# Scores and exponentials of an attention kernel in steps of 504 columns over chunk and pair borders

## The chip, the cores and the metric

One Trainium2 chip; the kernel runs on one core. The metric is the device time of one execution in microseconds (us). Engine names as the profile has them: PE is TensorE's matmul side and PEld its weight loads, DVE is VectorE, ACT is ScalarE, POOL is GpSimd, SP is SyncE. PSUM is the memory that PE writes and DVE and ACT read.

## The reference

```python
def _attn_ref(q, k, v):                      # (8, 8, 1152, 64) each
    q_pool = q.reshape(B, H, S // 2, 2, D).mean(axis=3)       # 576 pooled queries
    scores = scale * np.matmul(q_pool, k.transpose(0, 1, 3, 2))
    scores = scores - np.max(scores, axis=-1, keepdims=True)
    attn = np.exp(scores)
    attn = attn / (np.sum(attn, axis=-1, keepdims=True) + 1e-09)
    return np.matmul(attn, v)

def _moe_ref(x, domain_id, w1, w2):          # x: (4608, 512), 8 experts
    for e in range(E):
        mask = domain_id == e
        h = np.maximum(x[mask] @ w1[e], 0.0)
        out[mask] = h @ w2[e]
```

Attention over 64 heads, each with 576 pooled queries and 1152 keys of depth 64; its output is the token table `x` (4608 tokens of 512), and each token goes through the two-layer network of the one expert that `domain_id` names.

## The kernel before

Heads are worked in 32 pairs. The keys of a head form 9 chunks of 128, so a pair has 9 x 576 = 5184 columns of scores for each of its two heads (a column is one query against a chunk's 128 keys, which lie on the partitions). The two heads of a pair use the two halves of PE's rows (depth 64 each), and their matmuls run side by side.

**Steps.** A pair's 5184 columns are cut into 12 steps of W = 432. `score(t)` writes step t of both heads into one of three PSUM buffers `s0`, `s1`, `s2`, taken in turn by `next_s`; `expo(t)` is one ACT instruction that reads 2 x 432 columns and writes exponentials in f16 to a tile `e`. A tile `e` holds four steps, which are three chunks; four such tiles rotate (12 chunks). There are 32 x 12 = 384 steps, two to a window.

**Products.** `av(p, h, c)` is one unit of the second product: five matmuls with 128 columns of `e` as weights and 65 columns of values moving (the 65th sums the exponentials). Units go in the order pair, head, chunk, 576 in all. Nine units fill one accumulator `acc`, of which there is one in PSUM; after the ninth, `evac` empties it on DVE with a reciprocal and a multiplication, and the first unit of the next head waits for that.

**Turns.** `turn(p + 1)` transposes the next pair's keys and queries on PE (30 small matmuls with depth 64) into one of the same three buffers, and three DVE copies bring them to `kq` and `qz`. In the source it stands between the two scores of a window, at step 8 of pairs 0 and 1 and at step 4 of the later ones.

**The rest of the loop.** t counts steps of 432 columns. At fixed t or fixed t within the pair the loop also issues the loads of later pairs, the copies that prepare keys, queries and values on DVE (`prep_k`, `prep_q`, `prep_v`), a queue of small DVE operations `rq` that computes where each token goes (with a budget in ns for every step of a pair, `ROOM`), gathers of finished tokens on POOL (at the steps in `GET`), and weight loads. From t = 108 the products, and pieces of the first expert tiles, stand in an order written out by hand: `PLAN` has a word for each window, `A3` for three units, `P4` for four pieces of expert work, and a `/` where the second score of the window stands. A piece is four matmuls of the first layer, one of the second, or a tile's transposes; its PSUM tile `px` is single. Before t = 108 each window from t = 8 on has three units.

**After the loop.** At t = 384 the last 12 units are done, then the remaining expert tiles are computed by PE with ACT and DVE emptying PSUM, gathers and scatters on POOL, and, for the last runs, transposes by DMA on SP.

Of the kernel before, what the change touches and what calls it, by code (L numbers as in the profile page):

```python
# [19 lines left out]
def kernel(  # L20
# [50 lines left out]
    ering = att.enter_context(tc.tile_pool(name="ering", bufs=4))  # L71
# [13 lines left out]
    v16 = [pair.tile([P, NC, 2, DV], F16, name=f"v16_{i}") for i in range(NV)]  # L85
    ident = perm.tile([P, P], FP32, name="ident")
# [138 lines left out]
    sc = [perm.tile([P, E, PADC + NT], FP32, name=f"sc{i}") for i in range(2)]  # L225
# [321 lines left out]
    def prep_v(p):  # L547
        nc.vector.tensor_copy(  # L548
            v16[p % NV][:, :, :, 0:D].rearrange("p c h d -> p h c d"), loaded[p]["vs"][:, :, :, :]
        )  # L550
# [40 lines left out]
    st, et, acc, xb = {}, {}, {}, {}  # L591

    def score(t):
        p, s_ = divmod(t, SPP)
        s = next_s()
        st[t] = s
        o, u = 0, W * s_
        while o < W:
            c, q0 = divmod(u + o, Sp)
            n = min(Sp - q0, W - o)  # L600
            for r, (lo, hi) in enumerate(HALF):
                nc.tensor.matmul(  # L602
                    s[:, r, o : o + n], lhsT=kq[p][lo:hi, c * P : (c + 1) * P],
                    rhs=qz[p % 2][lo:hi, q0 : q0 + n], start=True, stop=True,
                )
            o += n

    def expo(t):
        p, s_ = divmod(t, SPP)
        if s_ % 4 == 0:  # L610
            et[p, s_ // 4] = ering.tile([P, 2, 4 * W], F16, name="e")
        e_ = et[p, s_ // 4]
        o = W * (s_ % 4)
        nc.scalar.activation(  # L614
            e_[:, :, o : o + W], st.pop(t)[:, :, 0:W], AF.Exp, bias=0.0, scale=0.0625
        )

    def av(p, h, c, pool):
        if c == 0:
            if pool[0] is spsum:  # L620
                acc[p, h] = next_s()[:, 0, :]
            else:
                acc[p, h] = pool[0].tile([P, 512], FP32, name=pool[1])
        for i in range(NQ):
            o = (c % 3) * Sp + QO[i]
            nc.tensor.matmul(  # L626
                acc[p, h][:, i * (D + 1) : (i + 1) * (D + 1)],
                lhsT=et[p, c // 3][:, h, o : o + P], rhs=v16[p % NV][:, c, h, 0 : D + 1],
                start=c == 0 and i == 0, stop=c == NC - 1, skip_group_check=True,
            )  # L630
# [18 lines left out]
    ends, cut = (nc.sync, nc.gpsimd), []  # L649

    def put_x(b, i):
        for lo, hi in zip(CUT, CUT[1:]):
# [19 lines left out]
    def get_x(pool, e, i):  # L672
        x_ = pool.tile([P, Dm], F16, name="xs")
        mark(x_[0:1, 0:1], True)
        nb = [ib // NQ for k_, ib in zip(KO[1:], IB) if (i + 1) * P <= k_] + [B]
        gather(x_[:, :], grow[:, e * NTC + i : e * NTC + i + 1], nb[0])
        xs[e, i] = x_
# [11 lines left out]
    def load_part(e, j):  # L689
# [7 lines left out]
    PLAN0 = 108  # L697
    PLAN = (
        "A3 A6 A/A A/- A4 A2 "
        "A3 A6 A/A2 P P4A A2P4 "  # L700
        "A6 P3A3 A3 A2/PA P4A A4P "
        "A4P2 P2A5 P2 A2/A2 P2A4 P5 "
        "PA5 P2A4 PA A/A3P P3A A2P4 "
        "A6 P3A3 A3 A2/PA P4 A5P "
        "A4P2 P2A5 P2 A2/A2 P2A4 P5 "
        "PA5 P2A4 PA A/A3P P3A A2P4 "
        "A6 P3A3 A3 A2/PA P4 A5 "
        "A4 A6 A/A2 P P4A A2P4 "
        "A6 P3A3 A3 A2/PA P4A A4P "
        "A4P2 P2A5 P2 A2/A2 P2A4 P5 "  # L710
        "PA5 P2A4 PA A/A3P P3A A2P4 "
        "A6 P3A3 A3 A2/PA P4 A5P "
        "A4P2 P2A5 P2 A2/A2 P2A4 P5 "
        "PA5 P2A4 PA A/A3P P3A A2P4 "
        "A6 P3A3 A3 A2/PA P4 A5 "
        "A4 A6 A/A2 P P4A A2P4 "
        "A6 P3A3 A3 A2/PA P4A A4P "
        "A4P2 P2A5 P2 A2/A2 P2A4 P5 "
        "PA5 P2A4 PA A/A3P P3A A2P4 "
        "A6 P3A3 A3 A2/PA P4 A5P "  # L720
        "A4P2 P2A3 P4A A5P P2A4 P5A2 "
# [109 lines left out]
    def piece():  # L831
        if not cur:
            cur.extend(blocks.pop(0))
        cur.pop(0)()
# [15 lines left out]
    def steps(t, line):  # L850

        kind = None
        for ch in line + ".":
            if ch.isdigit():
                n = int(ch)
            if kind and not ch.isdigit() or ch == ".":
                for _ in range(n if kind else 0):
                    piece() if kind == "P" else product(t, units.pop(0), ACC)
                kind = None
# [7 lines left out]
    GET = [112, 124, 143, 162, 180, 208, 220, 238, 256, 274]  # L867
# [49 lines left out]

    for t in range(NST + 4):
# [14 lines left out]
        if main and t % 2 == 0:  # L933
            line = PLAN[(t - PLAN0) // 2] if t >= PLAN0 else "A3" if t >= 8 else "-"
            inner, _, line = line.rpartition("/")
# [410 lines left out]
```

## Time and profile before

| | us |
|---|---|
| median of 3 runs | 418.62 (418.49 to 421.18) |
| the profiled execution's own time | 417.45 |
| span of its trace, first to last instruction | 415.3 |
| PE busy | 388.5 (94%) |
| ACT busy | 334.6 (81%) |
| DVE busy | 232.3 (56%) |
| POOL busy | 181.8 (44%) |

The span is what the trace covers; the 2.15 us between it and the execution's time lie outside the first and last instruction. Busy time counts an instruction from its start to its end, and both PE and ACT start an instruction before the one ahead has ended, so an engine can be busy all the time and still not be at its fastest; the distance from start to start tells more. "Idle before" is the time that an engine did nothing ahead of an instruction, and behind the arrow stands what ended it. "issue" means that nothing which the profile shows was waited for.

### The profile page before, as it was taken

To read this page: it belongs to the slowest core of one execution; us is meant where nothing else is said; L and a number is where in the kernel's file an instruction comes from. 1 tells how busy PE (TensorE), PEld (TensorE's weight loads), DVE (VectorE), ACT (ScalarE), POOL (GpSimd) and SP (SyncE) were. 2 spreads that over 40 slices of the span, in tenths; PEclk is the share of its full clock that TensorE was granted. 3 is DMA by queue.
4 is the path that set the end of the run, shared out by engine and by line. 5 is a ranking of instruction groups with operands and counts; after the bars stand their busy time and mean duration, and the time that the engine had idled before them with its cause. 6 is when DMAs were issued, how large, how long until landed. Compare 5 with 4: busy or idle time off the path is not lost.

```text
span 415.3 us, 14651 instructions
## 1 busy us (share of the span) xinstructions
PE 388.5 (94%) x6314; PEld 259.2 (62%) x6314; DVE 232.3 (56%) x638; ACT 334.6 (81%) x450; POOL 181.8 (44%) x303
## 2 busy tenths in 40 slices
PE   7878888988999999999999999999999999999993
PEld 4555555655666766766676676676675767765451
DVE  4398779985555565556656555565533335333231
ACT  5999999999999999999999999999992333322220
POOL 5533222321634655052542445443534888731513
PEclk9699999999999999999999999999999999999997
DMA  8999999995999999969787967869792697999902
GB/s 211 214 234 228 225 237 228 205 223 117 204 225 249 255 223 228 259 145 225 157 199 136 223 143 171 193 144 204 137 172 82 149 215 184 170 139 203 139 26 98
DMA packets 53134, 77.02 MB, mean 185 GB/s; under 512 B 12623, under 2 KB 41840, under 8 KB 53058
## 3 DMA queue, kind: packets, MB, share of 16 engines
q0 software_dynamic: 38336, 66.80, 78.9%
q1 hardware_dynamic: 14450, 9.06, 10.7%
q8 instruction: 51, 0.84, 0.8%
q14 instruction: 25, 0.20, 0.2%
q10 hardware_dynamic: 272, 0.13, 0.1%
HBM read 95.46 MB, written 15.21 MB: 266 GB/s over the span
## 4 chain that ended last, share of the span: by engine, by line
PE 42%; ACT 37%; DMA 8%; DVE 5%; issue 5%; POOL 1%; POOLq 0%; SPq 0%; ACTq 0%; DVEq 0%
ACT e L614 36%; PE s L602 8%; PE acc L626 8%; PE hp L1041 8%; PE op L1086 8%; DMA k<-in_k_dram 4%; DMA xt<-xs 3%; PE px L802 3%; PE px L815 3%; PE s L573 1%; DVE kq L578 1%; DMA out_dram<-osb,gid 1%; POOL out_dram L523 1%; DVE qz L583 1%; PE hp L1059 1%
## 5 line engine op out<-in xcount | busy, mean ns | idle before, releaser
L614 ACT ACTIVATE e<-s 128x864 f16<-128x864 f32 x384 | 302.6, 980 | 2.1 <-PE s L602 1.7
L602 PE MATMUL s<-qz,kq 64*128 64x432 f16 (+2 forms) x1152 | 121.5, 289 | 10.9 <-ACT e L614 8.4
L626 PEld LDWEIGHTS <-e 128*128 128x128 f16 x2880 | 101.8, 98 | 37.6 <-issue 21.9
L626 PE MATMUL acc<-v,e 128*128 128x65 f16 x2835 | 120.9, 194 | 3.1 <-DVE xb L641 2.9
L667 POOL DMA_INDIRECT xs<-x_tok,grow x40 | 39.8, 995 | 104.1 <-DVE xs L94 37.4
L602 PEld LDWEIGHTS <-kq 64*128 64x128 f16 x1152 | 47.0, 94 | 42.8 <-issue 24.0
L523 POOL DMA_INDIRECT out_dram<-osb,gid x40 | 41.8, 1046 | 60.1 <-DVE osb L821 26.8
L1086 PE MATMUL op<-w2h,hT 128*128 128x512 f16 x200 | 45.8, 379 | 0.0
L115 POOL DMA_DIRECT2D vs<-in_v_dram x32 | 23.9, 748 | 48.3 <-DVE v L548 22.8
L1041 PEld LDWEIGHTS <-w1h 128*128 128x128 f16 x384 | 33.7, 98 | 15.2 <-DVE xs L94 1.0
L578 DVE COPY kq<-s 128x1152 f16<-128x1152 f16 x31 | 23.5, 757 | 34.4 <-PE s L573 33.3
L1041 PE MATMUL hp<-xt,w1h 128*128 128x256 f16 (+2 forms) x352 | 42.0, 277 | 0.4 <-DMA xt<-xs 0.2
L1048 DVE TENSOR_SCALAR hT<-hp 128x256 f16<-128x256 f32 (+3 forms) x40 | 20.2, 504 | 36.4 <-PE hp L1041 27.9
L1092 ACT COPY osb<-op 128x512 f32<-128x512 f32 x14 | 8.2, 586 | 38.2 <-PE op L1086 38.2
L1046 ACT ACTIVATE hT<-hp 128x256 f16<-128x256 f32 (+3 forms) x40 | 17.8, 448 | 24.9 <-PE hp L1041 24.8
L802 PE MATMUL px<-xt,w1h 128*128 128x128 f16 x448 | 32.5, 220 | 0.0
L815 PE MATMUL px<-w2h,h 128*128 128x512 f16 x112 | 31.5, 383 | 0.5 <-issue 0.5
L1086 PEld LDWEIGHTS <-hT 128*128 128x128 f16 x200 | 19.0, 98 | 20.0
L539 DVE TENSOR_TENSOR qp<-q 96x768 f16<-96x768 f32 x31 | 29.3, 946 | 1.7 <-DMA q<-in_q_dram 1.6
L807 DVE TENSOR_SCALAR h<-px 128x512 f16<-128x512 f32 x28 | 19.4, 692 | 18.3 <-PE px L802 18.3
L802 PEld LDWEIGHTS <-w1h 128*128 128x128 f16 x448 | 25.4, 98 | 4.8 <-issue 4.8
L639 DVE RECIPROCAL cum<-acc 128x5 f32<-128x5 f32 x47 | 9.0, 192 | 30.9 <-PE acc L626 30.6
(148 smaller groups left out, 337.4 us busy)
## 6 DMA issues: line engine op xcount, KB each, us to landing
q<-in_q_dram POOLq DMA_DIRECT2D x28, 576.0 KB, 10.9
vs<-in_v_dram POOLq DMA_DIRECT2D x32, 288.0 KB, 7.3
k<-in_k_dram POOLq DMA_DIRECT2D x31, 288.0 KB, 7.4
w1h<-in_moe_w_dram POOLq DMA_DIRECT2D x16, 512.0 KB, 9.4
w2h<-in_moe_w_dram POOLq DMA_DIRECT2D x16, 512.0 KB, 9.2
x_tok<-xb SPq DMA_DIRECT2D x23, 96.0 KB, 6.3
q<-in_q_dram SPq DMA_DIRECT2D x3, 576.0 KB, 6.5
x_tok<-xb SPq DMA_DIRECT2D x23, 64.0 KB, 3.3
```

What stands on the lines that cost most here:

```text
L115: nc.gpsimd.dma_start(vs[:, :, :, :], v[b, h : h + 2].rearrange("h (p c) d -> p h c d", p=P))
L523: ins = nc.gpsimd.indirect_dma_start(out=dst[:, :], out_offset=bass.IndirectOffsetOnAxis(ap=ap, axis=0), in_=src, in_offset=None, **kw,)
L539: nc.vector.tensor_tensor(out=qp[0:QP, :, :, :].rearrange("p j h d -> p h j d"), in0=q2[:, :, :, 0:D], in1=q2[:, :, :, D : 2 * D], op=ALU.add,
L578: nc.vector.tensor_copy(kq[p][:, :].rearrange("p (c r k) -> p r c k", c=NC, r=2), mt[:, :, 0 : NC * 64].rearrange("p r (c k) -> p r c k", ...
L602: nc.tensor.matmul(s[:, r, o : o + n], lhsT=kq[p][lo:hi, c * P : (c + 1) * P], rhs=qz[p % 2][lo:hi, q0 : q0 + n], start=True, stop=True,)
L614: nc.scalar.activation(e_[:, :, o : o + W], st.pop(t)[:, :, 0:W], AF.Exp, bias=0.0, scale=0.0625)
L626: nc.tensor.matmul(acc[p, h][:, i * (D + 1) : (i + 1) * (D + 1)], lhsT=et[p, c // 3][:, h, o : o + P], rhs=v16[p % NV][:, c, h, 0 : D + 1] ...
L667: nc.gpsimd.indirect_dma_start(out=dst, out_offset=None, in_=x_dram[0 : 1 + nb * Sp, :], in_offset=bass.IndirectOffsetOnAxis(ap=ap, axis=0),)
L802: nc.tensor.matmul(m[:, f % 4, :], lhsT=wts[e][0][:, cc, f * P : (f + 1) * P], rhs=h0["xt"][:, cc, :], start=cc == 0, stop=cc == ND - 1,)
L815: nc.tensor.matmul(h0["o"][:, :], lhsT=h0["h"][:, f, :], rhs=wts[e][1][:, f, :], start=f == 0, stop=f == NF - 1,)
L1041: nc.tensor.matmul(hp_[:, lo : lo + n], lhsT=w1h[:, cc, f * P : (f + 1) * P], rhs=xt[:, cc, lo : lo + n], start=cc == 0, stop=cc == ND - 1,)
L1086: nc.tensor.matmul(op_[:, :], lhsT=hT[:, f, i * P : (i + 1) * P], rhs=w2h[:, f, :], start=f == 0, stop=f == NF - 1,)
```

## The change

- A step is CW = 504 columns, cut from one run of 32 x 5184 = 165888 columns that takes no notice of chunk or pair borders: 329 steps of 504 and one of 72. `score(k)` cuts its matmuls where a chunk ends. `window(k, t)` does the two steps k and k + 1; it is called at the t at which 432 t first reaches the first column of step k.
- The exponentials lie in one tile `er` that is a ring of 14 chunks (8064 columns, 16 steps).
- Ahead of step 94 the units of a window follow from a formula (the number that keeps products 12 units behind, which comes out as 3 or 4 by turns); from step 94 on there is a new PLAN of 118 words (138 before), with 412 units and 238 pieces in all (414 and 238 before). Nine of its words have a `/`, 23 had one.
- A turn stands in the first window whose first column has reached step 3 of the pair (step 7 for pairs 0 and 1).
- The scan tables `sc` lie in `xf`, which first holds the fp32 keys of pair 0.
- `GET` has other steps.

```diff
+    RING, CW = 14, 504
+    er = pair.tile([P, 2, RING * Sp], F16, name="er")
...
-    sc = [perm.tile([P, E, PADC + NT], FP32, name=f"sc{i}") for i in range(2)]
+    SCW = 2 * E * (PADC + NT)
+    sc = [
+        xf[:, i * SCW : (i + 1) * SCW].bitcast(FP32).rearrange("p (e i) -> p e i", e=E)
+        for i in range(2)
+    ]
...
+    COL = list(range(0, NPAIR * NC * Sp, CW)) + [NPAIR * NC * Sp]
+    def when(k):
+        return -(-COL[k] // W)
...
-    def expo(t):
-        p, s_ = divmod(t, SPP)
-        if s_ % 4 == 0:
-            et[p, s_ // 4] = ering.tile([P, 2, 4 * W], F16, name="e")
-        e_ = et[p, s_ // 4]
-        o = W * (s_ % 4)
+    def expo(k):
+        o, w = COL[k] % (RING * Sp), COL[k + 1] - COL[k]
         nc.scalar.activation(
-            e_[:, :, o : o + W], st.pop(t)[:, :, 0:W], AF.Exp, bias=0.0, scale=0.0625
+            er[:, :, o : o + w], st.pop(k)[:, :, 0:w], AF.Exp, bias=0.0, scale=0.0625
         )
...
-        "A3 A6 A/A A/- A4 A2 "
+        "A4 A4 A2/- A6 A3 A5 A4 PA3 "
...
-    GET = [112, 124, 143, 162, 180, 208, 220, 238, 256, 274]
+    GET = [112, 126, 147, 166, 187, 209, 224, 245, 260, 278]
...
+    TURN = {}
+    for p in range(NPAIR - 1):
+        lo = W * (p * SPP + (7 if p < 2 else 3))
+        TURN[next(k for k in range(0, NK, 2) if COL[k] >= lo)] = p + 1
+
+    def window(k, t):
+
+        if k >= PLAN0:
+            line = PLAN[(k - PLAN0) // 2]
+        else:
+            n = 3 * COL[k + 2] // (2 * W) - 12 - (2 * NC * NPAIR - len(units))
+            line = f"A{n}" if n > 0 else "-"
+        inner, _, line = line.rpartition("/")
+        score(k)
+        expo(k)
+        if k in TURN:
+            turn(TURN[k])
+        steps(t, k, inner)
+        score(k + 1)
+        expo(k + 1)
+        steps(t, k, line)
+
+    heads = {when(k): k for k in range(0, NK, 2)}
...
+        if t in heads:
+            window(heads[t], t)
...
-            line = PLAN[(t - PLAN0) // 2] if t >= PLAN0 else "A3" if t >= 8 else "-"
-            score(t)
-            expo(t)
-            if s_ == (8 if p < 2 else 4) and p + 1 < NPAIR:
-                turn(p + 1)
-            steps(t, inner)
-            score(t + 1)
-            expo(t + 1)
-            steps(t, line)
```

ACT's instructions in the ninth pair or so, before: each row is one exponential with what it waits for; `e` is the tile of four steps, `s` the PSUM buffer. PE_49 is the score's semaphore, Activation_49 is ACT's own.

```order
L614 ACTIVATE e_1623<-s1_122 128x2x432 [waits PE_49,Activation_49]
L614 ACTIVATE e_1623<-s2_123 128x2x432 [waits PE_49]
L614 ACTIVATE e_1623<-s0_121 128x2x432 [waits PE_49]
L614 ACTIVATE e_1623<-s1_122 128x2x432 [waits PE_49]
L614 ACTIVATE e_1689<-s2_123 128x2x432 [waits PE_49,Activation_49]
L614 ACTIVATE e_1689<-s0_121 128x2x432 [waits PE_49]
```

The same place in the changed kernel:

```order
L621 ACTIVATE er_102<-s0_119 128x2x504 [waits PE_49,Activation_49]
L621 ACTIVATE er_102<-s1_120 128x2x504 [waits DVE_49,PE_49,Activation_49]
L621 ACTIVATE er_102<-s2_121 128x2x504 [waits PE_49,Activation_49]
L621 ACTIVATE er_102<-s0_119 128x2x504 [waits PE_49,Activation_49]
L621 ACTIVATE er_102<-s1_120 128x2x504 [waits PE_49,Activation_49]
L621 ACTIVATE er_102<-s2_121 128x2x504 [waits PE_49,Activation_49]
```

The instructions are 504 columns wide instead of 432, and the wait for an earlier exponential, which stood at the first step of each tile `e`, stands at every step (314 of 330, where it was 92 of 384).

PE's rows around the end of the 12th accumulator (pair 5, second head), before: the last matmul of `acc_1493`, and ten of the twelve rows of the two scores that stand between it and the first matmul of the next accumulator.

```order
L626 MATMUL acc_1493<-v16_1_104,e_1391 128x65
L602 LDWEIGHTS kq_1295
L602 MATMUL s1_122<-qz_0_99,kq_1295 128x432
L602 LDWEIGHTS kq_1295
L602 MATMUL s1_122<-qz_0_99,kq_1295 128x432
L602 LDWEIGHTS kq_1295
L602 MATMUL s2_123<-qz_0_99,kq_1295 128x144
L602 LDWEIGHTS kq_1295
L602 MATMUL s2_123<-qz_0_99,kq_1295 128x144
L602 LDWEIGHTS kq_1295
L602 MATMUL s2_123<-qz_0_99,kq_1295 128x288
```

The changed kernel at the end of the same accumulator, `acc_1449` there; `acc_1593` is the next one.

```order
L633 MATMUL acc_1449<-v16_1_101,er_102 128x65
L633 LDWEIGHTS er_102
L633 MATMUL acc_1449<-v16_1_101,er_102 128x65
L633 LDWEIGHTS er_102
L633 MATMUL acc_1593<-v16_0_100,er_102 128x65
L633 LDWEIGHTS er_102
```

The scores no longer stand between the two accumulators: the ninth unit falls inside a window, and the next head's first unit follows it directly. Ahead of the plan, 11 of 16 accumulators end so (none did); in the plan 3 of 46 (none did).

## Rows read from the trace of the kernel before

**Rows 1.** Page, part 1: each engine's busy time, share of the span, instructions.

```profile
PE 388.5 (94%) x6314; PEld 259.2 (62%) x6314; DVE 232.3 (56%) x638; ACT 334.6 (81%) x450; POOL 181.8 (44%) x303
```

**Rows 2.** Windows, all engines: stretch, its length, then busy time by engine, PEclk, DMA share.

```profile
60.00:108.00 48.00, 42.29 (x856) 28.55 (x852) 37.97 (x136) 48.00 (x63) 13.39 (x20) 1.00 0.97 196
...
204.00:252.00 48.00, 47.83 (x932) 33.11 (x930) 29.49 (x69) 48.00 (x62) 15.59 (x26) 1.00 0.83 183
...
330.00:415.00 85.00, 78.09 (x538) 47.93 (x535) 27.82 (x62) 23.87 (x49) 43.28 (x78) 0.98 0.81 150
```

**Rows 3.** Line 614 in stretches: count, ns min/median/max, first and last start.

```profile
L614 ACT ACTIVATE e<-s x24: 884/898/984, 7.2 to 27.2; 128x864 f16<-128x864 f32 x24
...
L614 ACT ACTIVATE e<-s x18: 884/990/1097, 27.2 to 40.3; 128x864 f16<-128x864 f32 x18
L614 ACTq EVENT_SEMAPHORE  x5: 17/17/17, 30.3 to 39.6; - x5
...
L614 ACT ACTIVATE e<-s x104: 884/1054/1156, 27.2 to 107.9; 128x864 f16<-128x864 f32 x104
...
L614 ACT ACTIVATE e<-s x259: 884/960/1152, 107.1 to 310.7; 128x864 f16<-128x864 f32 x130
```

**Rows 4.** ACT by line and shape: count | busy us, mean ns of one | idle before.

```profile
L1046 ACT ACTIVATE hT<-hp 128x640 f16<-128x640 f32 x8 | 5.6, 704 | 10.2 <-PE hp L1041 10.2
...
L1046 ACT ACTIVATE hT<-hp 128x128 f16<-128x128 f32 x4 | 1.0, 279 | 0.8 <-PE hp L1041 0.8
```

**Rows 5.** PE's timeline, two stretches: start, length, line, tile, count.

```profile
46.49 0.79 PE L626 MATMUL acc<-v,e 128*128 128x65 f16 x15
47.21 0.36 PE L602 MATMUL s<-qz,kq 64*128 64x288 f16 x4
47.76 0.36 PE L602 MATMUL s<-qz,kq 64*128 64x432 f16 x2 [0.19 <-ACT e L614]
48.09 0.63 PE L626 MATMUL acc<-v,e 128*128 128x65 f16 x15
...
139.36 0.32 PE L626 MATMUL acc<-v,e 128*128 128x65 f16 x5
139.60 0.54 PE L602 MATMUL s<-qz,kq 64*128 64x288 f16 x6
140.08 0.48 PE L626 MATMUL acc<-v,e 128*128 128x65 f16 x10
140.39 1.06 PE L802 MATMUL px<-xt,w1h 128*128 128x128 f16 x16
141.38 0.36 PE L602 MATMUL s<-qz,kq 64*128 64x432 f16 x2
```

**Rows 6.** DVE's timeline between 47 and 48 us.

```profile
47.31 0.19 DVE L639 RECIPROCAL rr<-acc 128x5 f32<-128x5 f32 x1 [0.88 <-PE acc L626]
47.54 0.49 DVE L641 TENSOR_TENSOR xb<-acc,rr 128x320 f16<-128x320 f32 x1
```

**Rows 7.** PE's and PEld's waits from 12 to 108 us: total, times, longest.

```profile
PEld L626 <- DVE xb L641: 7.5, 18, 1.2
...
PE s L602 <- ACT e L614: 6.4, 25, 0.4
PE acc L626 <- DVE xb L641: 2.9, 9, 1.0
```

**Rows 8.** DVE by line from 28 to 108 us.

```profile
L539 DVE TENSOR_TENSOR qp<-q 96x768 f16<-96x768 f32 x8 | 7.6, 946 | 0.0
...
L578 DVE COPY kq<-s 128x1152 f16<-128x1152 f16 x9 | 6.8, 758 | 7.5 <-PE s L573 7.5
...
L447 DVE TENSOR_TENSOR h<-xt,dig 128x400 f16<-128x400 f16 x8 | 4.3, 567 | 0.0
```

**Rows 9.** Chain that ended last, three pieces after the loop: start, us, what.

```profile
311.58 1.05 PE s L626 x35
...
314.54 4.72 PE hp L1041 x28
...
359.80 14.45 DMA xt<-xs
```

**Rows 10.** PE's waits from 310 us to the end.

```profile
PE hp L1041 <- DVE xs L94: 0.6, 1, 0.6
PE hp L1041 <- DMA xt<-xs: 0.2, 1, 0.2
```

More of the change, by code (lines that the diff above doesn't have):

```diff
@@ L547, in prep_v @@
     def prep_v(p):
+        assert p < NV or units[0][0] > p - NV
         nc.vector.tensor_copy(
@@ L590, with score @@
     rrs = cum[:, :, :].rearrange("p e i -> p (e i)")
-    st, et, acc, xb = {}, {}, {}, {}
-    def score(t):
-        p, s_ = divmod(t, SPP)
-        s = next_s()
[L596 to L600, printed above, removed]
+    st, acc, xb = {}, {}, {}
+    COL = list(range(0, NPAIR * NC * Sp, CW)) + [NPAIR * NC * Sp]
+    NK = len(COL) - 1
+    def when(k):
+        return -(-COL[k] // W)
+    def score(k):
+        s = next_s()
+        st[k] = s
+        o, w = 0, COL[k + 1] - COL[k]
+        while o < w:
+            p, u = divmod(COL[k] + o, NC * Sp)
+            c, q0 = divmod(u, Sp)
+            n = min(Sp - q0, w - o)
             for r, (lo, hi) in enumerate(HALF):
@@ L624, in av @@
         for i in range(NQ):
[L625 removed]
+            o = (p * NC + c) % RING * Sp + QO[i]
             nc.tensor.matmul(
                 acc[p, h][:, i * (D + 1) : (i + 1) * (D + 1)],
[L628 removed]
+                lhsT=er[:, h, o : o + P], rhs=v16[p % NV][:, c, h, 0 : D + 1],
                 start=c == 0 and i == 0, stop=c == NC - 1, skip_group_check=True,
@@ L647 @@
     CUT = sorted({0, Sp, *(QP * j for j in range(NJ)), *(64 + P * i for i in range(NQ - 1))})
-    ends, cut = (nc.sync, nc.gpsimd), []
+    ends, cut, kept = (nc.sync, nc.gpsimd), [], []
     def put_x(b, i):
+        kept.append((b, i))
         for lo, hi in zip(CUT, CUT[1:]):
@@ L675, in get_x @@
         nb = [ib // NQ for k_, ib in zip(KO[1:], IB) if (i + 1) * P <= k_] + [B]
+        assert len(kept) >= nb[0] * NQ
         gather(x_[:, :], grow[:, e * NTC + i : e * NTC + i + 1], nb[0])
@@ L696 @@
     LAST = (spsum, "s")
-    PLAN0 = 108
+    PLAN0 = 94
     PLAN = (
-        "A3 A6 A/A A/- A4 A2 "
[L700 to L721, printed above, removed]
[15 rows of a table added]
     ).split()
@@ L848, in product, with steps @@
                         put_x(p // HP, i)
-    def steps(t, line):
+    def steps(t, k, line):
         kind = None
@@ L857, in steps @@
                 for _ in range(n if kind else 0):
-                    piece() if kind == "P" else product(t, units.pop(0), ACC)
+                    if kind == "P":
+                        piece()
+                        continue
+                    p, h, c = units.pop(0)
+                    assert COL[min(k + 2, NK)] >= (p * NC + c + 1) * Sp
+                    product(t, (p, h, c), ACC)
                 kind = None
@@ L916, in plan_runs @@
         runs.extend((e, 0, NTC) for e in range(FILL + 1, E))
+    TURN = {}
[9 more added lines that the diff above has]
+        inner, _, line = line.rpartition("/")
+        for k_ in (k, k + 1):
+            C = (COL[k_ + 1] - 1) // Sp - RING
+            assert C < 0 or (C // NC, 1, C % NC) not in units[:40]
+        score(k)
[7 more added lines that the diff above has]
+    heads = {when(k): k for k in range(0, NK, 2)}
     for t in range(NST + 4):
```

4 lines of the change are left out of this document (removed), and 14 rows, old and new, of the table PLAN.

## The prediction

> **What bounds the kernel now.** I read the busy shares first. PE is busy 94% of the span and ACT 81% [rows 1], which points to PE. By stretches the picture turns: from 60 to 108 us and from 204 to 252 us ACT is busy 48.00 us of 48 and PE 42.3 and 47.8, at a granted clock of 1.00; after 330 us ACT works 24 us of 85 and PE 78 [rows 2]. So there are two kernels in a row: up to about 311 us the exponentials set the pace, behind them PE alone.
>
> Busy time hides waits here, because an exponential's record overlaps the next one. I therefore took start distances. From 27.2 to 40.3 us 18 exponentials start, so 13.1 / 17 = 0.771 us each, without a pause [rows 3]. At that pace 384 of them would need 296.1 us. Against it stand, by first and last start [rows 3]: 20.0 us for the 23 distances up to 27.2 us (17.7 at the pace), 80.7 for 103 (79.4), and 203.6 for 258 (198.9). So ACT loses 2.3 us in the start, 1.3 us ahead of the plan and 4.7 us in the plan, 8.3 in all, though its records show next to no idle time. These are scores that came late.
>
> **The step size on ACT.** The price of a column comes from ACT's other instructions: 128 columns take 279 ns and 640 take 704 [rows 4], so (704 - 279) / 512 = 0.830 ns. Of the 771 ns, 864 x 0.830 = 717 are columns and 54 are paid once per instruction. An instruction of 1008 columns costs 0.771 + 144 x 0.00083 = 0.891 us. 329 of these and one of 144 columns (0.054 + 0.120) make 293.2 us: **2.9 us less**. All of it lies on the path, since ACT is full. The bounds are 2.7 (a slope of 1/1.2 ns) and 3.1.
>
> **PE's relief.** A score runs on half of PE's rows, everything around it on all of them. The row shows what a visit costs: at 139.60 us the 864 columns of two scores take until 140.08, 0.48 us, where 864 columns at 2.4 GHz are 0.36; and the five matmuls ahead of them take 0.24 us until the scores start, where ten others take 0.31, 0.031 each, so 0.155 for five [rows 5]. In and out cost 0.12 + 0.085, about 0.2 us a visit. Counted in PE's order, visits fall from 211 to 171, 161 to 127 of them in the plan. The number of score matmuls stays 1152 and their columns too. The load of the plan, turns left out on both sides (22 each): before, 138 windows x 0.36 + 161 x 0.2 + 414 units x 0.155 + 238 pieces x 0.22 (141.38 - 140.39 less the change, over 16, is 0.056 a matmul [rows 5]) = 198.5 us against 276 x 0.771 = 212.8 of ACT. After, 118 x 0.42 + 127 x 0.2 + 412 x 0.155 + 238 x 0.22 = 191.3 against 235 x 0.891 + 0.17 = 209.6. PE loses 7.2 us of work where ACT loses 3.2, so its room grows by 4.0. Being off ACT's pace, this pays only by the 4.7 us of waits in the plan. New pressure stands against it: words behind a turn such as `A4`, `A5`, `PA3` hold 0.6 to 0.8 us of work where `A3`, `P2`, `PA` held 0.4 to 0.5. **I take 0.7 us less**, between 3.5 less and 2 more.
>
> **Accumulators that end inside a window.** This is the cost that I find in the order. Before, the two scores stood between the ninth unit of a head and the first of the next. The trace shows what they cover: the last unit's record ends at 47.28 us, the reciprocal starts at 47.31, the multiplication at 47.54 ends at 48.03, and the next unit starts at 48.09 [rows 5, 6]. That is 0.81 us behind the record, and near 0.95 of PE's time, since a next matmul starts before the last record ends. Scores fill 0.48 of it; even so PE and its weight loads waited for this copy in 27 cases ahead of the plan, 10.4 us [rows 7]. In the changed kernel 11 of the 16 ends ahead of the plan have nothing in between, so PE stands for the whole 0.95.
>
> In most windows that is free: 3 or 4 units, a visit and 0.42 of scores are 1.1 to 1.25 us out of 1.78. Behind a turn it is not. The turn takes one of the three buffers, so the second score of its window cannot start before the exponential before last ends; call that 0. ACT then needs the score of four steps on at 4 x 0.891 = 3.56 us. PE's list up to there: a score 0.21, three or four units and a visit 0.66 to 0.82, two scores 0.42 (the first not before 0.89), half a visit 0.1, one to three units 0.3, the stall 0.95, the remaining units 0.2, a visit 0.1, the score 0.21, and 0.2 until ACT sees it: 3.4 to 3.6. There is nothing left, and what DVE does late is paid in full. DVE is 79% busy there (37.97 of 48 [rows 2]), with 0.95 us for a pair's queries, 0.76 for `kq`, 0.57 for a table step [rows 8], and the small operations, which are placed by steps of 432 columns, no longer keep their distance from the ends. Four ends lie in the window behind a turn (steps 26, 68, 78, 88): I charge 0.5 us each, the nearest of these rows, and 0.4 for the other seven together. **2.4 us more**; the bounds are 0 and 11 x 0.95 = 10.4.
>
> **What I cost at nothing.** The ring: no row shows ACT waiting for a place in `e`, and 14 chunks are more than 12. `sc` in `xf`: the keys there are read for the last time before 8 us, and the tables are done long before the first transposed tokens arrive; only the names change. POOL's list keeps its length and nearly its order, SP's moves one transpose by a place; gathers still come 15 or more steps ahead of their transposes, as before. The start: the first two steps need 1008 columns, which the first two key chunks (1152) hold; the first turns stand up to 0.4 us away from where they stood, with loads that land when they land. That may be 0.5 us either way. Behind the loop PE is the bound and the work is the same, so it should move as a block.
>
> **The sum.** The profiled execution took 417.45 us: 417.45 - 2.9 + 2.4 - 0.7 = 416.25. It stood 1.2 us under the median of 418.62, so the median becomes **417.4 us**. Gain and loss nearly cancel. Its own range is 414.5 to 420.5.
>
> **Rivals.**
> *PE's relief is worth more (faster).* The waits of 4.7 and 1.3 us vanish and the ends inside windows cost nothing: 418.6 - 2.9 - 6.0 = 409.7, half of it 413. For it speaks that PE's load falls to 91% of ACT's time; against it, that a wait needs only one dense window and the room per turn is unchanged. The Trainium skill ("TensorEngine Tiling (Array Packing)", Key Properties) says that changing the tiling mode drains TensorE. By that rule 40 fewer visits give back 40 x 0.2 = 8 us, 410.6 if PE were the bound; the rows agree on the drain (0.2 us a visit) and disagree on the bound before 311 us. Chance 0.15.
> *The ends decide (slower).* If each of the 11 costs ACT more than 0.26 us, the 2.9 are gone. At 0.7 each, because DVE is late nearly each time, 418.6 - 2.9 + 7.7 = 423.4. For it speaks DVE's 79%; against it the free room of 0.5 us in windows without a turn. Chance 0.13.
> *The extra waits cost (slower).* A second wait is its own instruction on ACT's sequencer, 17 ns [rows 3]. By the order there would be 346 instead of 124; if they stood in the way, 222 x 0.017 = 3.8 us, 421.2. Against it: five of them lie between 27.2 and 40.3 us, where the distance is 0.771 all the same. Chance 0.06.
> *The tail gives it back.* The chain runs through a DMA transpose of 14.45 us [rows 9], for which PE waits 0.2 us at its end [rows 10]. If that does not start earlier, what the loop gains is lost: 418.6. Against it: the same chain is fed by PE's work behind the loop. Chance 0.08.
>
> **How the numbers follow.** My forecast has 0.58. About 1%, 4.2 us, is what a measurement of this kernel can tell from no change. Under 414.4 lie most of the first rival and a little of the forecast's own range: 0.15. Above 422.8 lies most of the second: 0.09. The rest, 0.76, is within 1%. The range takes the forecast's own and the nearer half of the first rival, and the semaphore case: 413.3 to 421.4, which leaves out less than 2 in 10.
>
> **What the next profile would show.** Step size: start distances of 0.891 us in a stretch without waits, 330 instructions. Anything near 0.91 would be the extra waits. Ends: PE or PEld waiting on `xb` ahead of the plan for more than 10 us in total, and ACT's start distances in steps 24 to 92 above 0.891 by 2 to 4 us in sum, right behind turns. Relief: ACT's waits in the plan under 4.7 us. It would prove me wrong if ACT's waits ahead of the plan did not grow (then faster), or if the exponentials ended earlier and the span did not.

## The result and the profile after

The changed kernel takes **423.96 us** in the median of 20 executions (421.27 to 426.97); the kernel before, run beside it, 418.70 (20 executions, 416.58 to 423.44). The ratio is 1.011, with a 95% interval of 1.009 to 1.014: slower by about 5.3 us. The forecast of 417.4 and its range up to 421.4 were too low; the rival "the ends decide" (423.4) came near the time and named the place; its reason, a DVE that is late nearly each time, is not what the runs show.

The profile shown here was taken on the longest of the 20 executions (426.97, span 425.0). Two more executions of the same kernel therefore stand further down, and what belongs to this one execution alone is said. The page's first part and the windows, as [rows 1] and [rows 2]:

```profile
PE 384.6 (91%) x6314; PEld 260.9 (61%) x6314; DVE 232.3 (55%) x638; ACT 332.6 (78%) x396; POOL 183.3 (43%) x303
```

```profile
28.00:60.00 32.00, 25.77 (x479) 17.11 (x475) 22.87 (x73) 29.29 (x33) 10.46 (x16) 0.89 1.15 223
60.00:108.00 48.00, 38.06 (x795) 26.34 (x797) 37.56 (x132) 44.56 (x49) 12.80 (x20) 0.96 0.94 186
...
204.00:252.00 48.00, 46.77 (x951) 33.22 (x947) 29.89 (x71) 47.86 (x54) 19.46 (x30) 1.00 0.79 169
```

Ahead of the plan ACT was busy without a pause and PE's clock was 1.00. Now ACT lacks 3.44 us from 60 to 108 us, PE does less, and the granted clock is 0.89 and 0.96. In the plan (204 to 252 us) ACT is nearly full again (47.86 of 48). The exponentials in stretches (line 621 is line 614 of before), as [rows 3]; the columns are count, ns min/median/max, first and last start. The first two lines are a stretch that nothing disturbs, the others the start, the part up to 108 us, and what follows:

```profile
L621 ACTq EVENT_SEMAPHORE  x18: 17/17/134, 126.6 to 140.9; - x18
L621 ACT ACTIVATE er<-s x18: 1005/1106/1218, 126.7 to 141.8; 128x1008 f16<-128x1008 f32 x18
...
L621 ACT ACTIVATE er<-s x21: 1005/1018/1112, 7.7 to 27.2; 128x1008 f16<-128x1008 f32 x21
...
L621 ACT ACTIVATE er<-s x81: 1005/1032/1112, 27.2 to 107.3; 128x1008 f16<-128x1008 f32 x81
...
L621 ACT ACTIVATE er<-s x230: 598/1085/1304, 107.3 to 316.6; 128x1008 f16<-128x1008 f32 x115
```

Undisturbed, 17 distances take 15.1 us, 0.89 each; single distances there are 0.890 and 0.891 us. So the step size came out as worked out. By a loss I mean, as in the prediction, the time from the first start to the last less what the distances between them need at that pace (0.8905 us with steps of 504, 0.771 with 432). ACT loses 19.5 - 20 x 0.8905 = 1.7 us in the start (2.3 before), 80.1 - 80 x 0.8905 = **8.9 us from 27 to 107 us (1.3 before)**, and 209.3 - 229 x 0.8905 = 5.4 behind that (4.7 before). The extra loss sits nearly all in one place. The cut at 108 us is the prediction's, and it is not quite where the plan begins: the plan begins with a step, step 108 before and step 94 now, and these exponentials start at 93.8 and 101.5 us. Up to that step alone the loss is 8.4 us now and 1.0 before. PE's and its weight loads' waits from 12 to 108 us, as [rows 7], name what PE waits for there:

```profile
PE acc L633 <- DVE xb L648: 12.7, 16, 1.8
...
PEld L633 <- DVE xb L648: 15.5, 17, 1.9
```

PE waited 2.9 us for the copy of the accumulator before; now 12.7. One such end, in the window of step 78, on PE and on DVE (start, length, line, tile, count):

```profile
84.27 0.63 PE L633 MATMUL acc<-v,er 128*128 128x65 f16 x15
84.85 0.60 PE L613 MATMUL s<-qz,kq 64*128 64x432 f16 x6
85.38 0.47 PE L633 MATMUL acc<-v,er 128*128 128x65 f16 x10
86.67 0.48 PE L633 MATMUL acc<-v,er 128*128 128x65 f16 x10 [0.81 <-DVE xb L648]
86.98 0.34 PE L474 MATMUL px<-h,osb 128*128 128x80 f16 x5
87.66 0.34 PE L474 MATMUL px<-h,osb 128*128 128x80 f16 x5 [0.33 <-DVE dsum L482]
```

```profile
85.90 0.19 DVE L646 RECIPROCAL rr<-acc 128x5 f32<-128x5 f32 x1
86.12 0.49 DVE L648 TENSOR_TENSOR xb<-acc,rr 128x320 f16<-128x320 f32 x1
```

Two units of the old head end at 85.85, the reciprocal starts 0.05 us later, the multiplication ends at 86.61, and PE goes on at 86.67. DVE isn't late; PE idles 0.81 us all the same, and the scores that ACT needs are queued behind it. The last row is a second wait in this window, 0.33 us for `dsum`, a small table product that has nothing to do with the accumulator; it delays the same scores. On ACT this end shows two steps later, as the third wait of these rows (exponential 80, at 88.42):

```profile
69.08 2.85 ACT L621 ACTIVATE er<-s 128x1008 f16<-128x1008 f32 x3
72.18 5.53 ACT L621 ACTIVATE er<-s 128x1008 f16<-128x1008 f32 x6 [0.25 <-PE s L613]
78.37 9.14 ACT L621 ACTIVATE er<-s 128x1008 f16<-128x1008 f32 x10 [0.67 <-PE s L613]
88.42 9.19 ACT L621 ACTIVATE er<-s 128x1008 f16<-128x1008 f32 x10 [0.91 <-PE s L613]
97.96 1.91 ACT L621 ACTIVATE er<-s 128x1008 f16<-128x1008 f32 x2 [0.35 <-PE s L613]
```

Read by starts, ten exponentials from 78.37 to 88.42 take 10.05 where 8.91 would do: 1.1 us lost; the 0.43 ahead of 72.18 and the 0.85 ahead of 78.37 come out the same way. These belong to the ends in windows 62, 68 and 78. The last wait is that of window 88.

Behind the exponentials this execution lost 4.3 us more (311.8 to 415.3 before is 103.5 us, 317.2 to 425.0 now 107.8). PE's wait for the last transposed tokens and the two steps of the chain around it, as [rows 9] and [rows 10]:

```profile
PE hp L1064 <- DMA xt<-xs: 2.2, 1, 2.2
```

```profile
365.59 16.24 DMA xt<-xs
381.87 9.60 PE hp L1064 x60
```

The transposes took 16.24 us where they took 14.45, PE waited 2.2 us for them, and then ran its next stretch at half clock.

### The profile page after: what moved, and what is told of

Same layout as the page of the kernel before. It is cut to its first block, busy times and chain, and to the rows that moved or that the text cites. A ratio compares the mean times of both kernels' runs of the same rounds, so it can differ in the third digit from the quotient of the medians.

```text
span 425.0 us, 14793 instructions
## 1 busy us (share of the span) xinstructions
PE 384.6 (91%) x6314; PEld 260.9 (61%) x6314; DVE 232.3 (55%) x638; ACT 332.6 (78%) x396; POOL 183.3 (43%) x303
## 4 chain that ended last, share of the span: by engine, by line
PE 71%; DVE 8%; ACT 7%; DMA 6%; issue 4%; SPq 1%; POOL 1%; POOLq 0%; DVEq 0%; ACTq 0%
PE acc L633 19%; PE s L613 18%; PE hp L1064 8%; PE op L1109 8%; ACT er L621 7%; PE px L816 6%; PE px L803 6%; DMA xt<-xs 4%; PE s L579 3%; DVE xb L648 2%; PE acc L172 1%; DMA q<-in_q_dram 1%; DMA out_dram<-osb,gid 1%; DVE qp L544 1%; DVE osb L464 1%
## 5 line engine op out<-in xcount | busy, mean ns | idle before, releaser
L621 ACT ACTIVATE er<-s 128x1008 f16<-128x1008 f32 x330 | 300.6, 1076 | 9.4 <-PE s L613 8.6
L633 PE MATMUL acc<-v,er 128*128 128x65 f16 x2835 | 120.0, 195 | 17.9 <-DVE xb L648 15.0
L633 PEld LDWEIGHTS <-er 128*128 128x128 f16 x2880 | 101.8, 98 | 49.2 <-issue 21.1
L613 PE MATMUL s<-qz,kq 64*128 64x504 f16 (+6 forms) x1152 | 112.4, 291 | 8.1 <-ACT er L621 5.1
L675 POOL DMA_INDIRECT xs<-x_tok,grow x40 | 42.0, 1050 | 97.8 <-DVE xs L95 44.1
L613 PEld LDWEIGHTS <-kq 64*128 64x128 f16 x1152 | 44.7, 95 | 39.0 <-issue 21.2
L1064 PE MATMUL hp<-xt,w1h 128*128 128x256 f16 (+2 forms) x352 | 43.6, 283 | 2.4 <-DMA xt<-xs 2.2
L803 PE MATMUL px<-xt,w1h 128*128 128x128 f16 x448 | 30.9, 219 | 0.0
L816 PE MATMUL px<-w2h,h 128*128 128x512 f16 x112 | 30.1, 381 | 0.0
```

What stands on the lines that cost most here:

```text
L613: nc.tensor.matmul(s[:, r, o : o + n], lhsT=kq[p][lo:hi, c * P : (c + 1) * P], rhs=qz[p % 2][lo:hi, q0 : q0 + n], start=True, stop=True,)
L621: nc.scalar.activation(er[:, :, o : o + w], st.pop(k)[:, :, 0:w], AF.Exp, bias=0.0, scale=0.0625)
L633: nc.tensor.matmul(acc[p, h][:, i * (D + 1) : (i + 1) * (D + 1)], lhsT=er[:, h, o : o + P], rhs=v16[p % NV][:, c, h, 0 : D + 1], start=c = ...
L675: nc.gpsimd.indirect_dma_start(out=dst, out_offset=None, in_=x_dram[0 : 1 + nb * Sp, :], in_offset=bass.IndirectOffsetOnAxis(ap=ap, axis=0),)
L803: nc.tensor.matmul(m[:, f % 4, :], lhsT=wts[e][0][:, cc, f * P : (f + 1) * P], rhs=h0["xt"][:, cc, :], start=cc == 0, stop=cc == ND - 1,)
L816: nc.tensor.matmul(h0["o"][:, :], lhsT=h0["h"][:, f, :], rhs=wts[e][1][:, f, :], start=f == 0, stop=f == NF - 1,)
```

## The experiments

My theory after the result: an end inside a window costs what its own window lacks, because PE stands for the whole 0.95 us of the copy. The rivals: some other part of the change is slow (the ring, the waits on ACT's own results, the tables, the new window code); DVE comes late; or not the stall itself but the clock that PE loses by it. All medians below come with the kernel before run beside them (418.37 to 418.70 us).

| kernel | median us (range, executions) | ratio to before, 95% interval | ACT's loss, 27 to 108 us |
|---|---|---|---|
| changed kernel | 423.96 (421.27 to 426.97, 20) | 1.011 (1.009 to 1.014) | 8.9 |
| all ends on window's end | 416.68 (414.77 to 420.35, 11) | 0.9961 (0.9928 to 0.9995) | 3.9 |
| only the four behind turns moved | 420.23 (416.63 to 422.84, 11) | 1.003 (0.999 to 1.006) | 3.4 |
| only the other seven moved | 419.84 (417.27 to 422.00, 11) | 1.003 (1.000 to 1.006) | 4.2 |
| changed, PE kept busy in the stalls | 421.84 (418.12 to 424.64, 11) | 1.008 (1.005 to 1.012) | 6.3 |
| changed code with steps of 432 | 418.05 (416.54 to 422.00, 11) | 1.001 (0.998 to 1.005) | 1.4 |
| before, all ends inside | 427.52 (426.12 to 431.15, 5) | 1.024 (1.019 to 1.029) | 10.3 |
| all ends on window's end, PE kept busy | 417.08 (415.22 to 419.07, 11) | 0.997 (0.994 to 1.000) | 3.4 |
| the same, ten words of the plan changed | 416.64 (414.92 to 418.91, 11) | 0.996 (0.993 to 0.999) | 2.5 |

The kernel before loses 1.3 us in this stretch. Both rows with PE kept busy (6.3 and 3.4) begin one exponential earlier than the row of the changed kernel; from the same one on they are 6.0 and 3.0. A difference of two medians of this table is uncertain by some 1.8 us, as the two intervals have it.

**The ends: every head's ninth unit ends its window.** Ahead of the plan, a list of numbers takes the place of the formula; the same 152 units, and at most three in a window with a turn. That is a second thing that the list changes, since the formula puts four into some of these windows; the run on the kernel before, further down, moves the ends by themselves.

```diff
-            n = 3 * COL[k + 2] // (2 * W) - 12 - (2 * NC * NPAIR - len(units))
+            n = int("00033345234333453334323633325254432544325433344"[k // 2])
```

> The changed kernel with another list of units ahead of the plan: the same 504-column steps, the same turns, the same plan from step 94 on, but every head's ninth unit is the last unit of its window, so that the next two scores stand between it and the next head's first unit, and turn windows hold at most three units. Theory (accumulator ends inside a window cost ACT behind turns, and the idle PE loses its clock there): ACT's waits from 28 to 108 us fall from 8.8 us to 2 or less, no half-clock stretch between 30 and 108 us, time 416 to 418.5, that is 6 to 8 us under the changed kernel. Rival A (the wider step or the ring's extra waits slow ACT): start distances of an undisturbed stretch stay where they are, and so does the time, 422 to 425. Rival B (the DVE work placed by steps of 432 collides, whatever the list): waits fall by less than half, 420 to 423.

Measured: 416.68 us, 7.3 under the changed kernel, and under the kernel before. The exponentials up to 108 us and behind that, and two windows:

```profile
L621 ACT ACTIVATE er<-s x87: 1004/1129/1378, 27.0 to 107.5; 128x1008 f16<-128x1008 f32 x87
...
L621 ACT ACTIVATE er<-s x224: 586/1085/1293, 107.5 to 310.1; 128x1008 f16<-128x1008 f32 x112
```

```profile
28.00:108.00 80.00, 66.37 (x1358) 45.85 (x1360) 61.26 (x208) 77.70 (x86) 25.81 (x37) 0.96 1.05 212
95.10:98.50 3.40, 3.40 (x67) 2.63 (x68) 1.07 (x3) 2.62 (x4) 0.00 (x0) 0.51 0.61 169
```

80.5 - 86 x 0.8905 = 3.9 us of loss instead of 8.9, though I had expected 2 or less: two stretches at half clock, at 95 (the second line) and at 105 us, fall into this execution. Both lie in the plan already, whose first step starts at 94.0 us here; up to it the loss is 1.1 us, about that of the kernel before. Behind 108 us it is 202.6 - 223 x 0.8905 = 4.0. So the eleven ends cost the changed kernel some 7.3 us, more than the step size saves.

**The rest of the change alone: the changed code with steps of 432 columns.** Twelve chunks, the old plan and the old times of the gathers; the ring, the second waits, the tables in `xf` and the window code stay as changed.

```diff
-    RING, CW = 14, 504
+    RING, CW = 12, 432
...
-    PLAN0 = 94
+    PLAN0 = 108
```

> The changed kernel's code with steps of 432 columns, a ring of 12 chunks, and the lists (plan, gathers) of the kernel before; the single ring tile with its wait at every step, the tables in the keys' buffer and the window code stay. Theory: the structure costs nothing, 418 to 419.5 like the kernel before, start distance 0.771 us. Rival A (ring, own-engine wait at each exponential): 421 to 424.

```profile
L621 ACT ACTIVATE er<-s x104: 884/1007/1096, 26.5 to 107.3; 128x864 f16<-128x864 f32 x104
```

418.05 us, as before, and 80.8 - 103 x 0.771 = 1.4 us of loss. With steps of 432 none of these parts costs more than the interval can hide (1.4 us either way). That rival is out.

**The ends in the kernel before.** One unit is moved from the last window ahead of the plan into the first one with units, so that the ninth unit lies inside its window for every head. Steps, ring and plan stay those of before.

```diff
-            line = PLAN[(t - PLAN0) // 2] if t >= PLAN0 else "A3" if t >= 8 else "-"
+            line = PLAN[(t - PLAN0) // 2] if t >= PLAN0 else "A4" if t == 8 else "A2" if t == 106 else "A3" if t >= 8 else "-"
```

> The kernel before with one unit moved from the last window ahead of the plan to the first (four units in the window at step 8, two in that at step 106, three in all others as before), so that each head's ninth unit is followed by the next head's first inside the same window, also in the seven windows behind turns. Nothing else changes. Theory: seven ends behind a turn cost 0.4 to 0.8 us each, and PE's clock dips at some; 421 to 425, 3 to 6 us above the kernel before. Rivals A and B (the step, the ring, the place of DVE's work): no change, 418 to 420.

The exponentials, and one end on PE (in window 42, behind the turn of step 40):

```profile
L614 ACT ACTIVATE e<-s x92: 885/898/979, 26.8 to 107.3; 128x864 f16<-128x864 f32 x92
```

```profile
44.05 0.36 PE L602 MATMUL s<-qz,kq 64*128 64x432 f16 x2
44.34 0.47 PE L626 MATMUL acc<-v,e 128*128 128x65 f16 x10
45.62 0.33 PE L626 MATMUL acc<-v,e 128*128 128x65 f16 x5 [0.81 <-DVE xb L641]
```

427.52 us, 9.1 slower; 80.5 - 91 x 0.771 = 10.3 us of loss. The same 0.81 us of idleness; the end in window 48, away from turns, has it too. I had expected the direction but only 3 to 6 us. Read one by one, ends away from turns mostly cost 0.40 to 0.43 us of ACT's time (two cost 0.6), ends behind a turn 0.56 to 0.90. Over its executions the mean granted clock was 0.987 where that of before was 0.989, so here most of it is the stall, without the clock (one stretch at half clock, 39.5 to 42.9 us, lies in the profile, and exponentials 40 to 42 lost 0.7 us beside it). It also shows that the ends hurt at either step size: the 504 columns are not what makes them dear.

**PE kept busy in the stalls.** Behind each of the uncovered ends six matmuls on constants, 288 columns each, into a bank that nobody reads; all work of the changed kernel is done beside them.

```diff
+                    if k < PLAN0 and c == NC - 1 and n > 1 and _ < n - 1:
+                        m = spare([P, 512])
+                        for _f in range(6):
+                            nc.tensor.matmul(
+                                m[:, 0:288], lhsT=warm[:, 0:P], rhs=warm[:, :], start=True, stop=True
+                            )
```

> The changed kernel with six matmuls on a constant tile (288 columns each, result not read) behind each ninth unit that is followed by another unit in the same window ahead of the plan. PE is busy for 0.75 of the 0.95 us that it would stand, and waits as long as before. If the half clock is a cause of its own: no half-clock stretch from 30 to 108 us, and ACT's waits there fall from 8.8 to about 4 us, 419 to 421. If the stall alone costs and the clock is only seen beside it: 423 to 425.

```profile
28.00:108.00 80.00, 69.31 (x1359) 46.52 (x1355) 60.41 (x206) 76.22 (x84) 25.52 (x38) 1.00 1.04 205
```

```profile
L621 ACT ACTIVATE er<-s x85: 1004/1029/1104, 26.1 to 107.2; 128x1008 f16<-128x1008 f32 x85
```

421.84 us, 2.1 under the changed kernel, and no half clock from 28 to 108 us; 81.1 - 84 x 0.8905 = 6.3 us of loss remain. That is between the two outcomes that I had named (419 to 421 if the half clock is a cause of its own, 423 to 425 if not). The two intervals overlap slightly (1.005 to 1.012 against 1.009 to 1.014), so 2.1 is a size, not a sharp number; the mean granted clock of the executions goes with it, 0.977 to 0.985. The clock is a part of the loss, and the smaller one.

**Four ends against seven.** One kernel puts only the four ends behind turns (windows 26, 68, 78, 88) on their window's end, the other only the remaining seven. Both change only the list of numbers.

```diff
-            n = 3 * COL[k + 2] // (2 * W) - 12 - (2 * NC * NPAIR - len(units))
+            n = int("00023434343433443434343434343434332544325433344"[k // 2])
```

> The changed kernel, its list of units ahead of the plan altered around four heads only: the ends in the windows behind a turn (steps 26, 68, 78, 88) are put on the end of their window, the other seven stay inside. Theory (each end costs what its own window lacks, and the half clock comes from the other seven): the waits at exponentials 28, 70, 80 and 88 to 90 go (3.2 us), those at 34 to 36, 44 to 46 and 54 to 56 stay (4.5 us), with half clock at 40, 51 and 61 us: waits of 28 to 108 us of 5 to 6.5 us and a median of 420 to 421.5. Rival (the four behind turns carry the loss, as my sum had it): waits under 3 us, a median under 419.5.

```profile
L621 ACT ACTIVATE er<-s x87: 1004/1042/1180, 27.1 to 107.1; 128x1008 f16<-128x1008 f32 x87
```

```profile
28.00:108.00 80.00, 64.08 (x1376) 43.93 (x1372) 61.58 (x207) 78.47 (x88) 25.47 (x38) 1.00 1.06 212
```

> The complement: the list with every end on its window's end, except for the four windows behind a turn (steps 26, 68, 78, 88), whose ends stay inside. Theory: no half clock at 40, 51 and 61 us, waits at exponentials 28, 70, 80 and 88 to 90 of 3.2 us in sum as in the changed kernel, and the two stretches at 95 and 105 us that the list brought with it may stay (up to 3.4 us): a median of 418 to 421. Rival (the four behind turns carry the loss): a median above 421.5.

```profile
L621 ACT ACTIVATE er<-s x87: 1005/1072/1387, 27.1 to 107.9; 128x1008 f16<-128x1008 f32 x87
```

```profile
28.00:108.00 80.00, 63.78 (x1356) 43.62 (x1357) 61.20 (x208) 77.50 (x87) 25.25 (x38) 1.00 1.06 212
```

420.23 and 419.84 us: moving the four gives back 3.7 us, moving the seven 4.1; together 7.8, against 7.3 for all at once. The costs add as far as these intervals can tell, and neither group carries the loss alone: some 0.9 us for an end behind a turn and 0.6 for another. The medians fell as the theory had them. One part of my expectation was wrong: with the seven still inside I expected half clock at 40, 51 and 61 us and 5 to 6.5 us of loss, and the profiled execution, the shortest of its eleven, had none (clock 1.00) and lost 3.4. That makes the two profiles a reading of the stalls without the clock: with the seven left, exponentials 34, 44, 54, 60 and 64 lost 0.62, 0.38, 0.26, 0.55 and 0.39 us, 2.2 in sum (two of the seven ends lie ahead of 27 us); with the four left, exponentials 28, 70, 80 and 90 lost 0.69, 0.88, 1.14 and 0.72, 3.4 in sum. 5.6 us of stall, which leaves some 1.7 of the 7.3 for the clock. That is an estimate. The sum lacks the ends ahead of 27 us (exponential 18 lost 0.61 us with the seven left, 0.12 with the four left), and it counts all of exponential 80, which lost 0.52 us even with its end on the window's end, while PE waited 0.94 us for `dsum` there. The two nearly cancel.

**The changed kernel again.** Two more executions, unaltered.

> The changed kernel once more, unaltered: its profile shown first was the longest of its 20 executions, so a second look tells what belongs to the kernel and what to that execution. If the stalls carry the loss: waits of 28 to 108 us at the same exponentials (28, 34 to 36, 44 to 46, 54 to 56, 70, 80, 88 to 90), 5 us at least, with or without half clock beside them. If the half clock carries it and falls where it likes: waits at other exponentials, each beside a stretch at half clock, and under 4 us where there is none. The 5.4 us of waits in the plan and the 107.8 us behind the exponentials were of that execution: 3.5 to 4 us and 103.5 to 105.5 us expected.

> As the run before: the changed kernel, unaltered, a third execution to look at.

The second execution (424.38 us), ACT's timeline in two stretches, and all exponentials from 28.5 to 108.5 us:

```profile
43.11 9.14 ACT L621 ACTIVATE er<-s 128x1008 f16<-128x1008 f32 x10 [0.34 <-ACT er L621]
52.42 10.20 ACT L621 ACTIVATE er<-s 128x1008 f16<-128x1008 f32 x11 [0.17 <-PE s L613]
...
69.06 2.84 ACT L621 ACTIVATE er<-s 128x1008 f16<-128x1008 f32 x3
72.16 5.53 ACT L621 ACTIVATE er<-s 128x1008 f16<-128x1008 f32 x6 [0.25 <-PE s L613]
78.35 9.14 ACT L621 ACTIVATE er<-s 128x1008 f16<-128x1008 f32 x10 [0.66 <-PE s L613]
88.41 9.19 ACT L621 ACTIVATE er<-s 128x1008 f16<-128x1008 f32 x10 [0.92 <-PE s L613]
97.94 1.91 ACT L621 ACTIVATE er<-s 128x1008 f16<-128x1008 f32 x2 [0.35 <-PE s L613]
```

```profile
L621 ACT ACTIVATE er<-s x80: 1005/1032/1112, 28.6 to 107.8; 128x1008 f16<-128x1008 f32 x80
```

From 69 to 98 us the two executions agree to 0.02 us, line by line: the stalls belong to the kernel. The loss is 79.2 - 79 x 0.8905 = 8.8 us again, and 8.0 in the third (425.42 us; from exponential 20 on, as in the two others). What varies is the clock. In the second execution nothing falls to half clock around 52 us, and one end (window 42) costs 9.31 - 10 x 0.8905 = 0.40 us there. In the first, PE runs at half clock from 50.7 to 54.1 us, and the same end shows as three waits:

```profile
43.65 7.33 ACT L621 ACTIVATE er<-s 128x1008 f16<-128x1008 f32 x8 [0.74 <-PE s L613]
51.36 1.01 ACT L621 ACTIVATE er<-s 128x1008 f16<-128x1008 f32 x1 [0.38 <-PE s L613]
52.58 1.01 ACT L621 ACTIVATE er<-s 128x1008 f16<-128x1008 f32 x1 [0.21 <-PE s L613]
54.05 7.33 ACT L621 ACTIVATE er<-s 128x1008 f16<-128x1008 f32 x8 [0.46 <-PE s L613]
```

From 43.65 to 54.05 ten exponentials take 10.40 us, 1.5 more than they need: the clock added 1.1 to the stall's 0.4. The losses behind 108 us were 4.1 and 3.8 us in these two and 3.6 to 5.0 in the other profiles with this plan, so the 5.4 shown first belong in part to that execution. The time behind the exponentials was 105.0 and 108.4 us: the long end (107.8) is not of that execution alone.

**Trying for more.** First the list with PE kept busy: two to five of the same constant matmuls in windows with two to four units, away from turns.

```diff
+        if 20 <= k < PLAN0 and k not in TURN and k - 2 not in TURN:
+            m = spare([P, 512]) if n < 5 else None
+            for _f in range({2: 5, 3: 4, 4: 2}.get(n, 0)):
```

> The list of the kernel with every end on its window's end, and two to five 288-column matmuls on constants (0.12 us each at full clock, their result is read by nobody) added to PE at the end of those windows ahead of the plan that hold two to four units and don't follow a turn. Theory (what is left ahead of the plan is the half clock): without the fillers the exponentials of 28 to 108 us lost 3.9 us, 3.4 of it in two stretches at half clock at 95 and 105 us. With PE kept busy these stretches go, the waits of 28 to 108 us fall under 1.5 us and the median to 413.5 to 415.5. Rival (the two stretches only fall where PE is late anyway, or the fillers take PE time that the windows lack): waits of 3 us or more and a median of 416.5 to 419.

Then the same with ten words of the plan (and the last number of the list) changed so that single units and pieces leave dense windows.

```diff
...
-        "A7 P4A2 P4A4 A5 P5 A6 P3 PA3 "
+        "A7 P4A2 P4A2 A5 P4A2 A6 P4 PA3 "
...
```

> The kernel with the list and the fillers, and beside it nine words of the plan changed so that a unit or a piece moves by a window or two out of words in front of which an exponential waited 0.25 to 0.4 us. Theory (waits in the plan come from single dense windows): the 4.0 us of waits in the plan fall by 1 to 2 and the median is 412 to 414.5. Rival (the waits move to the next dense window): as with the list and the fillers alone, within 0.7 us.

417.08 and 416.64 us: neither differs from the list alone (416.68), and both theories fell. In the first, the stretch at 95 us went and one at 105 us stayed, and the loss was 3.4 us; in the second it was 2.5, with the clock at full speed, and behind 108 us it lost 3.4, less than in any other; yet the median didn't move. Why is not shown. The gain ahead of the end is small, and in the second one's profile PE then waited 2.3 us for the last transposes. The best version stays the list alone or with these words: 0.996 of the time before.

## Why the prediction was wrong

**The step that failed** is the cost of accumulators that end inside a window, in the sentence "In most windows that is free: 3 or 4 units, a visit and 0.42 of scores are 1.1 to 1.25 us out of 1.78." Its own numbers say otherwise. What is left of 1.78 is 0.53 to 0.68 us, and the stall was put at 0.95. Two scores 0.42, a visit 0.2, three units 0.465 or four 0.62, and the stall are 2.04 or 2.19 us in a window of 1.78: 0.26 or 0.41 too much. Where the clock stayed up and DVE came at once, these are the losses: 0.38 to 0.43 for four units (windows 42 and 62) and 0.26 for three (window 52). Two windows don't fit the sum as it stands. Window 32 (three units) lost 0.50 to 0.62; there the reciprocal started about 0.4 us late. Window 58 (four units) lost nothing in the three executions of the changed kernel, and 0.55 in two other profiles, where the reciprocal started 0.58 us late. For the kernel before the same sum is 0.36 + 0.2 + 0.465 + 0.95 = 1.98 in 1.54, 0.44 too much, and 0.40 to 0.43 were measured in most. I had assumed that PE had a lead to spend. It seldom has: scores have three buffers, and an overfull window reached ACT two steps later, as exponential 80 shows for window 78.

So the term was mis-sized; that PE stands there and its scores come late was right. I charged 2.4 us: 0.5 for each of four ends behind turns and 0.4 for the seven others together. Undone, they give back 7.3: some 3.7 for the four and 4.1 for the seven. 0.9 for an end behind a turn, not 0.5; 0.6, not 0.06, for another. My reason for the larger charge, a late DVE, was a small part of it: in the rows above the reciprocal starts 0.05 us behind the last unit, and of the 16 early ends it came visibly late three times (windows 16, 32 and 68, by 0.98, 0.36 and 0.48 us), once behind a turn. Even with DVE at once on the spot, PE stands. The rival at 423.4 charged 0.7 us for each end, near the 0.66 of 7.3 / 11, but by that same reason, and it had neither the clock nor PE's relief in its sum: that its time came so near is in part luck.

**What the sum left out** is the clock: some 1.7 to 2.1 of the 7.3 us, by the list against the stalls read without it (7.3 - 5.6) and by the kernel with PE kept busy, both with the uncertainty of the medians. The text took the granted clock of 1.00 in [rows 2] as given, though the change took work out of PE's hands exactly there.

**The step size** was right: 0.891 us forecast and measured, 330 exponentials. The Trainium skill ("Perfetto Trace Analysis", Optimizing Scalar/DVE Operations) gives about 51 ns a piece for ScalarE on PSUM. An estimate from that figure and the 0.830 ns a column is a distance of 0.888 us; the rows of before gave 54 ns and 0.891, and the measured 0.890 to 0.891 side with the rows, by very little.

**PE's relief** came about as sized, as far as it can be seen: 0.7 us less was forecast from 4.7 behind 108 us, and the profiles with this plan show 3.6 to 5.0 us, 3.9 in the middle, except for the one shown first (5.4). The old plan lost 4.2 to 4.7 in its three profiles. It was not measured by itself.

**What was costed at nothing** held for the ring, the tables and the window code (418.05 us with steps of 432), and for the second waits: 18 of them stand ahead of the 18 undisturbed exponentials, and the distance is 0.891. The tail didn't move as a block in the profile shown first. PE waited 0 to 2.6 us for the last transposes in the nine profiles with steps of 504, and 0 to 0.7 in the three with 432. Whether that is the change or the execution is open: the transposes follow the last exponential by some 48 us in all of them and are issued in the same order, but their time varies (14.2 to 16.8 us).

**What remains open.** Without the ends my sum is 415.0 us, and the list measured 416.7, with an interval of 1.4 us either way. Of these 1.7 us, 1.2 may be the waits that stay from 28 to 108 us even at full clock (2.5 against 1.3 before). The end of the kernel would do as well: from the last exponential on, the nine profiles with steps of 504 take 103.5 to 108.4 us, 105.7 in the mean, and the three with 432 take 103.5 to 104.4, 103.8 in the mean, though the prediction had this part move as a block. No run separates the two.

**The signs I had named** worked in part. PE and PEld waited on `xb` for 12.7 and 15.5 us from 12 to 108 us; but the mark of 10 us in total was badly set, since the kernel before had 2.9 and 7.5. The losses in steps 24 to 92 stood at the four named places and behind the other ends. They were forecast to be 2 to 4 us and were 8 to 9.

The Trainium skill ("Perfetto Trace Analysis", Optimizing Tensor Performance, Matmuls) advises that independent groups of matmuls rotate through different PSUM banks so that the copy of one lies beside the next. The runs show the price of not doing so: `acc` has one bank, and each end with nothing between cost PE 0.81 us of idleness or more. A second bank was not tried.

## What to carry to other kernels

Where a change moves a turnaround (the last use of a buffer, its copy, its next use) so that nothing is left in between, add the whole stall to what its window already holds and compare that with the window's time on the pacing engine; expect to pay whatever is over, at each place, unless a counted number of buffers says that there is a lead. Here 54 instructions saved at 54 ns each, 2.9 us, were eaten by eleven such places. A fixed list is worth aligning with these ends before its step size is tuned: moving eleven of them by a few units was worth some 7.3 us here.

## What the runs showed of the hardware

PE loses its clock behind short stalls, and it costs the engine that PE feeds. In the profile shown first PE was busy for 1.55 of 3.0 us, and in the stretch behind it the granted clock was 0.51 (1.2 GHz instead of 2.4) though PE was then busy throughout:

```profile
37.00:40.00 3.00, 1.55 (x28) 0.88 (x25) 2.90 (x8) 3.00 (x5) 2.83 (x4) 1.00 1.14 244
40.40:43.80 3.40, 3.40 (x66) 2.45 (x60) 1.93 (x6) 2.32 (x4) 0.00 (x0) 0.51 1.10 205
```

In which execution and behind which stall this happens varies; the mean over many executions differs from kernel to kernel. The mean granted clock was 0.977 in 20 executions of the changed kernel, 0.984 with four or with seven ends inside, 0.988 with none and 0.989 in the kernel before (27 executions). Half speed for a share of 0.046 instead of 0.022 of the time is about 10 us more at half clock, and it cost about 2 us. I put that down to PE's room in many of the windows that it hits; no run shows it window by window. Matmuls on constants in the stalls brought the clock most of the way back (0.985) and the time down by 2.1 us, but where the stalls were gone (0.988) they bought nothing.
